# Two quarters of the first Q, K, V projection at new widths, and two attention chunks turned by DMA one phase earlier

## The chip, the cores and the metric

The kernel runs on one core of a Trainium2 chip. A time is device microseconds (us) of one execution of the whole program on that core; a kernel's time is the median of several executions. The engines of the core are named as the profile names them: TensorE is PE, with its weight loads listed apart as PEld; VectorE is DVE; ScalarE is ACT; GpSimd is POOL; SyncE, which here only issues DMAs, is SP. POOL issues DMAs too. Each engine takes its instructions in the order in which they were issued, and waits for the data of the one at its head.

## What is computed

A layer of local, dilated attention (32 heads of 20, eight keys at distances 0, 2, ..., 14) times a gate from a feed-forward network, on a sequence of 2048 rows of 640 in float32:

```python
def reference(A_x, A_wqkv, A_wo, B_x, B_w1, B_w2):
    x = A_x                                   # 1 x 2048 x 640
    xn = _layernorm(x)
    # s: Q, K, V = xn @ wqkv; 32 heads of 20; each row attends to rows
    #    pos - 0, 2, ..., 14; softmax over these eight; result @ wo
    s = _A_ref(xn, A_wqkv, A_wo)
    # _B_ref: silu(xn @ w1) @ w2, with 1536 hidden
    g = _silu(_B_ref(xn, B_w1, B_w2))
    return x + s * g
```

## The kernel before

**Tiling.** The 2048 rows are worked in four groups of 512, g = 0 to 3: two halves of the sequence, and in each the even and the odd rows, since keys lie at even distances. A group is four tiles of 128 tokens (t = 0 to 3). 640 inputs are five K-chunks of 128 (c = 0 to 4). Float32 products are made of three matmuls each: every operand is split into a rounded part (hi) and the rest (lo), and PE computes hi x hi, lo x hi and hi x lo (L971 to L973 in the projection, L1016 and L1018 for products with two column parts of 384 and 256, L1143 to L1145 for `w1`).

**A group's two phases.** In the *Q, K, V phase* (`qkv_phase`) PE makes the projection in four quarters q of eight heads: each is 5 chunks x 4 tiles x 3 = 60 matmuls into four accumulator banks, as wide as the quarter's columns. A quarter's own columns are 160 of Q, 160 of K and 160 of V, 480 together. In the groups g = 1 to 3 the quarters 0, 1 and 2 take 32 columns each of quarter 3's Q besides, so their widths are 512, 512, 512 and 384; in g = 0 all four are 480 wide. Function `parts` says which columns a quarter takes. ACT reads the banks out (`evac_qkv`: keys and values L749, Q L752, the 32 further columns L755), SP shifts keys and values along the rows (`halo`, L767, L777, L779), and DVE makes the scores (L792, L795) and the weighted values (L826, L831, L834) of the attention, which runs on into the next phase. In the *FFN phase* (`ffn_phase`) PE makes `w1` blocks (`up`) and `w2` blocks (`down`) in turn, and somewhere in it the product of the **previous** group's attention with `wo` (`wo_phase`), whose banks DVE reads out by multiplying them into the gate (L1048) before a block of `w2` can use them. The same phase loads the next group's rows of `x` (L615), takes their statistics (L622, L624) and normalizes them (L634).

**Weights.** Seven weight tiles `w` are used in a ring. At first use a weight comes raw from memory by SP (`raw_load`, L546), ACT makes the hi part (L581), POOL or DVE the lo part (L585), and for later groups both halves are stored to memory (L589); from then on POOL loads them in one DMA (L572). The store of quarter 3 of g = 0 is cut: 32-column pieces go to the halves of quarters 0 to 2, since the later groups use them there.

**Turning the attention's output.** `wo_phase` needs the attention's output O with its columns on the partitions. A chunk c of 128 columns is turned by PE, or by DMA in `turn_o`: *send* is a copy on ACT that parts the halves of each word (L676) and two DMA transposes on SP (L680); *join* puts them together on ACT (L689), makes hi on ACT (L693) and lo on DVE (L694). The table `ON_DMA` says for each group which chunks go by DMA, at which quarter of the next Q, K, V phase send and join are issued, and how many us behind by the planner's clock. A send needs two tiles of 128 x 512 to work in: `LENT` lends it the key and value tiles KV[1], KV[2], KV[3] for chunks 1, 2 and 3, between the use of one group and the next (`spare`, `lend`); chunk 0 uses the tiles `turn` and `sf`. Chunks of the next group's x are turned in the same way in the FFN phase (`turn_x`).

**What sets the order.** All operations are handed to a planner (`Weave`) with their reads and writes, a cost from its own table, a priority (mostly the clock of PE when they were handed over) and sometimes an earliest time. It plays them through and fixes one order for each engine; `emit` issues that. So an edit at one place moves instructions at others. The names of the tables that the change touches are `LENT`, `IN_PARTS` and `ON_DMA`; `QAT` is the column at which a ring tile of g = 0's projection begins.

## Time and profile before

| what | us |
| --- | --- |
| median of 3 runs (623.55 to 623.58) | 623.56 |
| the profiled execution | 624.1 |
| its span, first to last instruction | 622.3 |
| PE busy in it | 617.2 |
| DVE busy | 540.7 |
| ACT busy | 272.7 |
| POOL busy | 114.8 |
| granted TensorE clock, mean | 1.000 |

The span is what the trace shows, from the first instruction to the last; the rest of an execution's time lies around it. Busy times of engines overlap, so they do not add up. A timeline row of the profile gives the start in us from the span's begin, the length in us, the engine, the line of the kernel's text, the operation, the tiles that it writes and reads, their shapes and how often it came in a row; in brackets stands how long the engine had been idle before it and for whom it waited. SPq and POOL's DMA rows show the issuing of a transfer, not its landing.

### The profile page before, as it was taken

What the parts mean: (1) busy time and instruction counts of PE and PEld (TensorE: products, weight loads), DVE (VectorE), ACT (ScalarE), POOL (GpSimd) and SP (SyncE); (2) the same over time, 40 slices, a digit from 0 to 9 for tenths busy, and PEclk for the clock granted to TensorE, in tenths of its full rate; (3) what the DMA queues carried; (4) which work ended last, traced back from release to release, by engine and by line L of the source; (5) the groups of instructions that cost most, each with busy time, mean ns of one, the idle gap of its engine ahead of it and who ended that gap; (6) DMA issues with size and microseconds to landing.
All of it is one profiled execution on the core that took longest, in us unless ns stands there. A gap on an engine that the chain in (4) does not pass through costs nothing.

```text
span 622.3 us, 9038 instructions
## 1 busy us (share of the span) xinstructions
PE 617.2 (99%) x3395; PEld 557.9 (90%) x3395; DVE 540.7 (87%) x545; ACT 272.7 (44%) x496; POOL 114.8 (18%) x165
## 2 busy tenths in 40 slices
PE   9999999999999999999999999999999999999997
PEld 7888999998889998999888999989988999999997
DVE  6599899999788998998948499899996999899834
ACT  5445555364545225453545521625654272252220
POOL 5800000011110142111221015121222211111100
PEclk9999999999999999999999999999999999999999
DMA  9999999599999999965999999998499999987552
GB/s 297 305 319 317 323 377 364 220 326 269 278 298 309 331 237 321 272 198 140 203 219 262 344 363 330 295 230 252 137 225 286 240 321 304 295 241 243 189 191 86
DMA packets 105114, 167.39 MB, mean 269 GB/s; under 512 B 36605, under 2 KB 66781, under 8 KB 105069
## 3 DMA queue, kind: packets, MB, share of 16 engines
q1 hardware_dynamic: 78573, 87.08, 52.8%
q0 software_dynamic: 25952, 79.31, 46.6%
q8 instruction: 27, 0.44, 0.3%
q10 hardware_dynamic: 544, 0.41, 0.2%
q14 instruction: 18, 0.15, 0.1%
HBM read 107.91 MB, written 34.16 MB: 228 GB/s over the span
## 4 chain that ended last, share of the span: by engine, by line
PE 98%; DMA 0%; DVE 0%; issue 0%
PE acc L1016 22%; PE acc L1018 15%; PE acc L973 10%; PE acc L971 10%; PE acc L972 10%; PE rot L1144 9%; PE rot L1145 9%; PE rot L1143 9%; PE acc L909 2%; PE rot L644 1%; DMA xin<-in_A_x_dram 0%; PE rot L893 0%; PE rot L1129 0%; DVE st L878 0%; PE rot L852 0%; DVE gate L1097 0%
## 5 line engine op out<-in xcount | busy, mean ns | idle before, releaser
L1016 PE MATMUL acc<-w,sh 128*128 128x384 f32 x384 | 113.4, 334 | 0.0
L971 PE MATMUL acc<-w,th 128*128 128x512 f32 (+2 forms) x300 | 112.9, 376 | 0.0
L973 PE MATMUL acc<-w,th 128*128 128x512 f32 (+2 forms) x300 | 112.8, 376 | 0.0
L972 PE MATMUL acc<-w,tl 128*128 128x512 f32 (+2 forms) x300 | 112.8, 376 | 0.0
L1018 PE MATMUL acc<-w,sh 128*128 128x256 f32 x384 | 107.3, 279 | 0.0
L792 DVE TENSOR_TENSOR pr<-q,kv 128x2560 f32<-128x2560 f32 x32 | 90.3, 2822 | 16.0 <-DMA kv<-kv 15.7
L826 DVE TENSOR_TENSOR pr<-q,kv 128x2560 f32<-128x2560 f32 x32 | 94.5, 2954 | 0.7
L1143 PE MATMUL rot<-th,w 128*128 128x512 f32 x240 | 94.2, 393 | 0.0
L1145 PE MATMUL rot<-th,w 128*128 128x512 f32 x240 | 93.8, 391 | 0.0
L1144 PE MATMUL rot<-tl,w 128*128 128x512 f32 x240 | 93.7, 391 | 0.0
L795 DVE TENSOR_REDUCE l<-pr 128x128 f32<-128x2560 f32 x32 | 90.1, 2815 | 0.3
L1156 ACT ACTIVATE sh<-rot 128x512 fp32r<-128x512 f32 x48 | 28.8, 600 | 139.7 <-PE rot L1145 139.5
L572 POOL DMA_DIRECT2D w<-half_q x52 | 37.4, 719 | 234.4 <-DVE pr L831 97.2
L572 POOL DMA_DIRECT2D w<-half_w x72 | 38.6, 536 | 202.7 <-PE acc L1018 87.9
L831 DVE TENSOR_TENSOR pr<-pr 128x1280 f32<-128x1280 f32 x64 | 74.0, 1156 | 1.3
L1018 PEld LDWEIGHTS acc<-w,sh 128*128 128x128 f32 x384 | 72.2, 188 | 1.1 <-DVE gate L1048 0.3
L1016 PEld LDWEIGHTS acc<-w,sh 128*128 128x128 f32 x384 | 72.1, 188 | 0.9
L972 PEld LDWEIGHTS acc<-w,tl 128*128 128x128 f32 x300 | 56.3, 188 | 8.8
L973 PEld LDWEIGHTS acc<-w,th 128*128 128x128 f32 x300 | 56.3, 188 | 8.7
L971 PEld LDWEIGHTS acc<-w,th 128*128 128x128 f32 x300 | 56.3, 188 | 8.7
L1016 PE MATMUL acc<-w,sl 128*128 128x384 f32 x192 | 57.9, 333 | 0.0
L749 ACT ACTIVATE kv<-acc 128x320 f32<-128x320 f32 x64 | 27.5, 441 | 60.9 <-PE acc L973 59.5
(115 smaller groups left out, 1037.8 us busy)
## 6 DMA issues: line engine op xcount, KB each, us to landing
w<-half_w POOLq DMA_DIRECT2D x72, 640.0 KB, 6.6
w<-half_q POOLq DMA_DIRECT2D x39, 512.0 KB, 5.5
half_w<-w SPq DMA_DIRECT2D x24, 640.0 KB
kv<-kv SPq DMA_DIRECT2D x15, 560.0 KB
w<-half_wo POOLq DMA_DIRECT2D x10, 640.0 KB, 8.0
kv<-kv SPq DMA_DIRECT2D x15, 420.0 KB
gate<-in_B_w_dram SPq DMA_DIRECT2D x16, 320.0 KB
w<-half_q POOLq DMA_DIRECT2D x13, 384.0 KB, 7.6
```

The source lines that it names most:

```text
L572: add("POOL", 1.0, lambda: nc.gpsimd.dma_start(both, src), [("half", u), ("half", u, "more")], [kh, kl], due + 10, nbytes=2 * n * P * 4)
L792: dve(2560, lambda t=t: nc.vector.tensor_tensor(out=PR, in0=win(qq[:, t:t + 2, :], W, 0), in1=win(kv[:, 0, t:t + 2, :], W, CQ), op=OP.mult ...
L795: dve(2560, lambda t=t: nc.vector.tensor_reduce(out=l[:, t:t + 2].rearrange("p t w h -> p (t w h)"), in_=PR.rearrange("p t w (h d) -> p (t ...
L826: dve(2560, lambda t=t, v=v: nc.vector.tensor_tensor(out=PR.rearrange("p t w (h d) -> p t (w h) d", d=DH), in0=e[:, t:t + 2].rearrange("p ...
L971: nc.tensor.matmul(o, hi, wh, start=c == 0, stop=False)
L972: nc.tensor.matmul(o, lo, wh, start=False, stop=False)
L973: nc.tensor.matmul(o, hi, wl, start=False, stop=c == DC - 1)
L1016: nc.tensor.matmul(a[t][0][:, :CA], st, w[:, :CA], start=first, stop=last)
L1018: nc.tensor.matmul(b[t // 2][0][:, h * CB:(h + 1) * CB], st, w[:, CA:], start=first and h == 0, stop=last, skip_group_check=True)
L1143: nc.tensor.matmul(h, wh[:, cs], TH[i][:, c, :], start=c == 0, stop=False)
L1144: nc.tensor.matmul(h, wh[:, cs], TL[i][:, c, :], start=False, stop=False)
L1145: nc.tensor.matmul(h, wl[:, cs], TH[i][:, c, :], start=False, stop=c == DC - 1)
```

## The change

Four things are changed.

1. In the first group the third quarter takes 32 columns of the last quarter's Q, so its widths are 480, 480, 512 and 448. `parts` and `evac_qkv` say so; `SLOT` gives where the 32 columns lie (the first slot of quarter 3's Q tile is now that of quarter 2). Raw loads of these two quarters become two DMAs for each of five chunks (the 32 or 128 Q columns apart); the stores of 32-column pieces fall from nine to six, and the start column `QAT` holds for quarters 0 and 1 alone. ACT has four more readouts of 32 columns.
2. `LENT` becomes a table by group: for the attention that is joined in g = 2 chunk 0 is lent KV[0] in place of `turn` and `sf`.
3. `EARLY_O`: the send of chunks 0 and 1 of g = 1's attention, which was issued at the beginning of g = 2's Q, K, V phase, is issued in g = 1's FFN phase behind its `wo_phase`, no earlier than 48 and 56 us after the planner's clock there; `ON_DMA` now has only their joins, at quarter 0 instead of quarter 1.
4. `IN_PARTS` 3: in the last group the third tile of `x` for the residual is loaded in two DMAs. The argument `NG` in place of `g` in the last group's `turn_o` selects the same tiles as before.

```diff
-LENT = None, 1, 2, 3, None
+LENT = {2: (0, 1, 2, 3, None)}
+EARLY_O = {1: ((0, 48.0), (1, 56.0),)}
-IN_PARTS = 2
+IN_PARTS = 3
+SLOT = 1, 2, 0
@@ parts(i)
-        if i >= first_q:
-            if q < NQ - 1:
-                cols.append(((NQ - 1) * CQ + q * MORE, MORE))
-            else:
-                cols[0] = (q * CQ + q * MORE, CQ - q * MORE)
+        if q == NQ - 1:
+            gone = MORE * (NQ - 1 if i >= first_q else 1)
+            cols[0] = (q * CQ + gone, CQ - gone)
+        elif i >= first_q or q == NQ - 2:
+            cols.append(((NQ - 1) * CQ + SLOT[q] * MORE, MORE))
@@ start(i)
-        return QAT if i < first_q else 0
+        return QAT if i < 2 * DC else 0
@@ raw_load(k)
-            if i >= first_q:
+            if len(cols) > 3 or q == NQ - 1:
@@ turn_o
-        lent = LENT[c] if g < NG - 1 else None
+        lent = LENT[g][c] if g in LENT else None
@@ evac_qkv
-        skip = MORE * q if g and q == NQ - 1 else 0
+        skip = MORE * (q if g else 1) if q == NQ - 1 else 0
-        if g and q < NQ - 1:
+        if q < NQ - 1 and (g or q == NQ - 2):
+            slot = SLOT[q]
             act(MORE, lambda: nc.scalar.activation(
-                Q[NQ - 1][:, t, q * MORE:(q + 1) * MORE], ps[:, 3 * CQ:], AF.Copy), [kp], [("q", NQ - 1, t, q)], 0)
+                Q[NQ - 1][:, t, slot * MORE:(slot + 1) * MORE], ps[:, 3 * CQ:], AF.Copy), [kp], [("q", NQ - 1, t, slot)], 0)
@@ ON_DMA
-              NG - 2: ({0: ((0, 0, 4.0), (1, 0, 4.0)), 1: ((0, 1, 8.0), (1, 1, 8.0), (2, 0, 0.0), (3, 0, 10.0)), 2: ((2, 1, 4.0),), 3: ((3, 1, 0.0),)},
+              NG - 2: ({0: ((0, 1, 2.0), (1, 1, 4.0)), 1: ((2, 0, 0.0), (3, 0, 10.0)), 2: ((2, 1, 4.0),), 3: ((3, 1, 0.0),)},
@@ ffn_phase, behind wo_phase
                     for v in sorted(set(lent)):
                         lend(*v, True)
+                    for c, at in EARLY_O.get(g, ()):
+                        turn_o(g + 1, c, ix, True, False, clock[0] + at)
```

PE's order keeps its rows; only the widths of 120 matmuls differ. A row below is line, operation, tile written and tile read, and the shape. The lines of the changed text are higher by 1 to 5.

SP in the Q, K, V phase of g = 2, from the first shift of quarter 0's keys (kv_93 to kv_96 are the quarters 0 to 3) on. Before:

```order
L767 DMA kv_93<-kv_93 112x2x640
L767 DMA kv_93<-kv_93 15x2x640
L767 DMA kv_93<-kv_93 112x2x480
L680 DMA_TRANSPOSE sf<-turn 128x4x128
L767 DMA kv_93<-kv_93 14x2x480
L777 DMA kv_94<-carry_121 1x2x640
L680 DMA_TRANSPOSE kv_96<-kv_96 128x4x128 x2
```

Of the change:

```order
L770 DMA kv_93<-kv_93 112x2x640
L770 DMA kv_93<-kv_93 15x2x640
L770 DMA kv_93<-kv_93 112x2x480
L770 DMA kv_93<-kv_93 14x2x480
L780 DMA kv_94<-carry_121 1x2x640
L782 DMA kv_94<-carry_121 2x2x480
L682 DMA_TRANSPOSE kv_96<-kv_96 128x4x128 x2
```

The transpose of chunk 0 that stood between the shifts is gone; those of chunk 3 (kv_96) stay.

The same queue at that phase's end, with the loads of `x` for g = 3 (xin) and raw loads of `wo` (xr). Before:

```order
L767 DMA kv_95<-kv_95 112x2x480
L767 DMA kv_95<-kv_95 14x2x480
L777 DMA kv_96<-carry_121 1x2x640
L779 DMA kv_96<-carry_121 2x2x480
L546 DMA xr_107<-in_A_wo_dram 128x640
L615 DMA xin<-in_A_x_dram 128x640
L546 DMA xr_108<-in_A_wo_dram 128x640
L615 DMA xin<-in_A_x_dram 128x640 x3
L589 DMA half_wo_167<-w_77 128x1280
```

Of the change:

```order
L617 DMA xin<-in_A_x_dram 128x640
L780 DMA kv_96<-carry_121 1x2x640
L782 DMA kv_96<-carry_121 2x2x480
L770 DMA kv_95<-kv_95 112x2x640
L770 DMA kv_95<-kv_95 15x2x640
L770 DMA kv_95<-kv_95 112x2x480
L770 DMA kv_95<-kv_95 14x2x480
L617 DMA xin<-in_A_x_dram 128x640 x3
L548 DMA xr_107<-in_A_wo_dram 128x640
L591 DMA half_wo_167<-w_77 128x1280
L548 DMA xr_108<-in_A_wo_dram 128x640
```

One load of `x` moved ahead of quarter 2's shifts (kv_95), the other three ahead of both raw loads.

DVE at the beginning of g = 2's FFN phase, from the normalization to the gate on `wo`. Before:

```order
L634 TENSOR_SCALAR xin<-xin,mv,sd 128x640 x4
L792 TENSOR_TENSOR pr<-q_98,kv_94 128x2560
L795 TENSOR_REDUCE l_104<-pr 128x128
L792 TENSOR_TENSOR pr<-q_98,kv_94 128x2560
L795 TENSOR_REDUCE l_104<-pr 128x128
L1048 TENSOR_TENSOR gate<-acc_113,gate 128x384
```

Of the change:

```order
L636 TENSOR_SCALAR xin<-xin,mv,sd 128x640 x4
L1161 TENSOR_TENSOR sl_87<-sf,sh_84 128x512
L795 TENSOR_TENSOR pr<-q_98,kv_94 128x2560
L587 TENSOR_TENSOR w_81<-xr_108,w_81 128x640
L798 TENSOR_REDUCE l_104<-pr 128x128
L829 TENSOR_TENSOR pr<-q_97,kv_93 128x2560
L834 TENSOR_TENSOR pr<-pr 128x2x640
L834 TENSOR_TENSOR pr<-pr 128x2x320
L837 TENSOR_TENSOR o<-pr 128x2x160
L829 TENSOR_TENSOR pr<-q_97,kv_93 128x2560
L1051 TENSOR_TENSOR gate<-acc_113,gate 128x384
```

One of the two score pairs of quarter 1 moved ahead of the normalization, and two products of quarter 0's values, the first with its sums, ahead of the gate.

SP in the first group, where quarters 2 and 3 are loaded raw. Before:

```order
L546 DMA xr_108<-in_A_wqkv_dram 128x3x160
L767 DMA kv_93<-kv_93 112x2x480
L767 DMA kv_93<-kv_93 14x2x480
L546 DMA gate<-in_A_wqkv_dram 128x3x160 x2
L546 DMA xr_107<-in_A_wqkv_dram 128x3x160
```

Of the change:

```order
L548 DMA xr_108<-in_A_wqkv_dram 128x3x160
L550 DMA xr_108<-in_A_wqkv_dram 128x32
L770 DMA kv_93<-kv_93 112x2x480
L770 DMA kv_93<-kv_93 14x2x480
L548 DMA gate<-in_A_wqkv_dram 128x3x160
L550 DMA gate<-in_A_wqkv_dram 128x32
L548 DMA gate<-in_A_wqkv_dram 128x2x160
L550 DMA gate<-in_A_wqkv_dram 128x128
L548 DMA xr_107<-in_A_wqkv_dram 128x2x160
L550 DMA xr_107<-in_A_wqkv_dram 128x128
```

Each load of the two quarters now has a smaller one behind it.

More of the change, by code (lines that the diff above doesn't have):

```diff
@@ L1213, in ffn_phase @@
                     for c in range(2):
-                        turn_o(g, c, io, True, True)
+                        turn_o(NG, c, io, True, True)
                     free_for(XP, [("xin", t, c) for t in range(T) for c in (0, CA)])
```

## The prediction

> **What bounds the kernel now.** I read the page's busy shares and chain first, then tables by stretch for TensorE (PE), then its waits, then the queues that feed the one stall that they show. Groups are counted g = 0 to 3.
>
> ```profile
> span 622.3 us, 9038 instructions
> PE 617.2 (99%) x3395; PEld 557.9 (90%) x3395; DVE 540.7 (87%) x545; ACT 272.7 (44%) x496; POOL 114.8 (18%) x165
> PE 98%; DMA 0%; DVE 0%; issue 0%
> ```
>
> PE is busy in 617.2 of 622.3 us and is 98% of the chain that ended last. So a gain must come from matmuls that take less time, or from the few gaps between them; work on other engines counts only where PE waits for it. The profiled execution took 624.1 us, 1.8 more than its span, and the median of the runs is 623.56; I work out differences inside the span and put them on the median.
>
> **First term, the widths.** These are four stretches of the table by windows for PE alone (start:end, length, busy and count, granted clock, DMA share, GB/s), each one quarter of a Q, K, V phase with 60 matmuls: 480, 512, 512 and 384 columns.
>
> ```profile
> 47.89:60.85 12.96, 12.96 (x62) 1.00 1.10 316
> 158.29:171.89 13.60, 13.60 (x62) 1.00 1.30 290
> 310.44:324.04 13.60, 13.60 (x61) 1.00 1.43 224
> 337.64:348.07 10.43, 10.43 (x62) 1.00 1.20 296
> ```
>
> Per matmul that is 12.96/60 = 216.0 ns at 480, 226.7 at 512 and 173.8 at 384. From 384 to 512 a column costs 52.9/128 = 0.413 ns; on that line 480 would take 213.5, so the measured 216.0 lies 2.5 ns above it. The change puts 512 and 448 in place of 480 and 480, for 60 matmuls each. The 512 is measured in the other groups. For 448 no row exists. On the line between 384 and 512 it takes 200.2 ns (12.01 us); with the surplus of 480 it takes 202.7 (12.16 us). The pair before is 25.92 us; after, 13.60 + 12.01 = 25.61 or 13.60 + 12.16 = 25.76, a gain of 0.31 or 0.16. If what makes 480 slow belongs to the first group and not to the width, 512 pays it too and the gain is 0. I take 0.23, midway between the first two, since the 512 and 384 of the other groups both lie on one line, and keep 0 to 0.31.
>
> [...]
>
> **Second term, a stall in the third group.** The next table, by windows for all engines, has three blocks of 72 `w2` matmuls, the first from g = 1 and the others from g = 2; then one row of the waits of PE's weight loads, and PE's timeline.
>
> ```profile
> 245.30:255.63 10.33, 10.33 (x73) 10.33 (x72) 10.26 (x9) 8.65 (x10) 3.43 (x4) 1.00 1.09 240
> 375.99:387.04 11.05, 11.01 (x74) 10.75 (x73) 10.98 (x11) 2.19 (x3) 7.35 (x9) 1.00 1.08 353
> 397.25:407.58 10.33, 10.33 (x73) 10.33 (x72) 10.19 (x7) 4.08 (x5) 1.59 (x3) 1.00 1.17 226
> ```
>
> ```profile
> PEld acc L1018 <- DVE gate L1048: 0.3, 1, 0.3
> 377.15 0.33 PE L1016 MATMUL acc<-w,sh 128*128 128x384 f32 x1
> 377.52 0.38 PE L1018 MATMUL acc<-w,sh 128*128 128x256 f32 x1
> ```
>
> Equal work takes 10.33 us twice and 11.05 once, so 0.72 us is lost after 375.99. At 377.15 to 377.52 the pipeline breaks because an accumulator bank is not yet free: VectorE (DVE) must first read the `wo` result out of it (the gate, L1048). The rest of the 0.72 is a slower pitch until the block's end; it began with the break, and I count it to it. Why is the gate late? DVE's timeline (start, length, operation, and in brackets idle time before it):
>
> ```profile
> 328.40 2.83 DVE L792 TENSOR_TENSOR pr<-q,kv 128x2560 f32<-128x2560 f32 x1 [10.07 <-DMA kv<-kv]
> 351.79 0.49 DVE L622 BATCH_NORM_STATS2 st<-xin 128x6 f32<-128x320 f32 x1 [4.83 <-DMA xin<-in_A_x_dram]
> 356.72 0.89 DVE L622 BATCH_NORM_STATS2 st<-xin 128x6 f32<-128x320 f32 x2 [1.58 <-DMA xin<-in_A_x_dram]
> 358.51 0.67 DVE L1158 TENSOR_TENSOR sl<-sf,sh 128x512 fp32r<-128x512 f32 x1
> 359.23 1.51 DVE L585 TENSOR_TENSOR w<-xr,w 128x640 fp32r<-128x640 f32 x2
> 360.86 2.25 DVE L634 TENSOR_SCALAR xin<-xin,mv,sd 128x640 f32<-128x640 f32 x4
> 371.59 2.82 DVE L795 TENSOR_REDUCE l<-pr 128x128 f32<-128x2560 f32 x1
> 374.33 3.14 DVE L1048 TENSOR_TENSOR gate<-acc,gate 128x384 f32<-128x384 f32 x6
> 378.06 2.81 DVE L826 TENSOR_TENSOR pr<-q,kv 128x2560 f32<-128x2560 f32 x1
> 381.40 2.34 DVE L831 TENSOR_TENSOR pr<-pr 128x1280 f32<-128x1280 f32 x2
> 383.77 0.49 DVE L834 TENSOR_TENSOR o<-pr 128x320 f32<-128x320 f32 x1
> ```
>
> DVE stood idle 10.07 us for the shifted keys of quarter 0 and 4.83 and 1.58 us for the next group's rows of `x`; its order then puts two scores (L792, L795) between the normalization (L634) and the gate. Both waits come from the one queue of SyncE (SP):
>
> ```profile
> 311.10 3.44 SPq L767 DMA_DIRECT2D kv<-kv  x3
> 314.58 1.91 SPq L680 DMA_TRANSPOSE sf<-turn  x1
> 316.54 1.53 SPq L767 DMA_DIRECT2D kv<-kv  x1
> 339.94 2.51 SPq L767 DMA_DIRECT2D kv<-kv  x2
> 344.30 0.69 SPq L615 DMA_DIRECT2D xin<-in_A_x_dram  x1
> 347.85 0.33 SPq L546 DMA_DIRECT2D xr<-in_A_wo_dram  x1
> 348.22 2.75 SPq L615 DMA_DIRECT2D xin<-in_A_x_dram  x3
> ```
>
> A transpose of attention chunk 0 stands ahead of the last shift of quarter 0 (316.54), which lands some 10 us after its issue ends. The `x` loads stand behind a raw load of `wo` at 347.85.
>
> The change takes the transposes of chunks 0 and 1 out of this phase, so the four shifts stand together, and its new order has all four `x` loads ahead of that raw load. I follow both chains. *Shifts:* without L680's 1.91 us the fourth ends its issue near 315.9. Its landing has no row; before it took 328.40 - 318.07 = 10.3 us, so it is at latest near 326.2 if that stays, earlier as fewer transposes are in flight. *Loads of x:* the first is now ahead of quarter 2's shifts, the other three right behind them. Those end at 342.45, so the three are issued by 342.45 + 2.75 = 345.2 instead of 350.97. DVE, waiting, began the first tile's statistics 6.8 us behind its issue's end (351.79 - 344.99); with that the last tile's run from 352.0 to 352.9, and with a weight split (0.75) and a few operations under half a us the normalization starts near 354.5 instead of 360.86. *Behind it,* by the new order, come L634 2.25, one L1158 0.67, scores 2.83 and 2.82 with a split 0.75 between, values 2.81, 2.34, 0.49, 2.81: 17.8 us. The gate starts near 372.3. It must start by about 374.33 - 0.72 - 0.23 = 373.4 if PE, itself 0.23 earlier, is not to wait. That holds with 1.1 us to spare, so the term is 0.72, with 0 as its lower bound if that slack is used up.
>
> **The rest at nothing.** Moved, not removed, are two ScalarE (ACT) copies, four transposes, two joins on ACT and two subtractions on DVE; PE's count stays. They now share the DMA engines with the weight loads of g = 1's FFN. The ring of seven weight tiles, loaded as each comes free, hides that; PE's waits name no DMA. If that cover were gone, a load behind one transpose could cost PE up to the 1.91 us of its issue. The third `x` load of the last group in two parts (IN_PARTS) lies long ahead of its use. At the end of the last value product DVE's L1158 goes ahead of both L831:
>
> ```profile
> 590.58 0.60 ACT L855 ACTIVATE th<-rot 128x512 fp32r<-128x512 f32 x1 [2.81 <-PE rot L852]
> 591.21 0.69 DVE L856 TENSOR_TENSOR tl<-rot,th 128x512 fp32r<-128x512 f32 x1 [0.53 <-ACT th L855]
> ```
>
> DVE waits there 0.53 us for ACT, so a delay of up to 0.5 hides; I allow 0 to 0.15.
>
> **Sum.** -0.23 - 0.72 = -0.95, so 623.56 - 0.95 = **622.6 us** (-0.15%). With both terms at their best -1.03; a change of under 0.2% (1.25 us, about what a measurement of this kernel can tell from none) is the likeliest.
>
> **Rivals.** *The stall stays.* If the three `x` loads issue or land over 1.1 us later than I say, part of the 0.72 stays; wholly, only the widths pay: 623.3. For it speaks the thin slack. If the shifts land no earlier than 328.40, the new order is worse than the old: 47 us of DVE work (the new order's operations at their durations before) stand between that score and the gate, it starts at 375.4, and PE loses 1.1 more: 624.4. Against that speaks the transpose gone from the queue.
>
> [...]
>
> *Slower: the first group's loads.* Quarters 2 and 3 of g = 0 come raw from memory, now in two DMAs for each of ten K-chunks. ACT takes what it does in order, and its evacuation of PE's banks stands behind a weight copy:
>
> ```profile
> 33.32 0.61 ACT L581 ACTIVATE w<-gate 128x480 fp32r<-128x480 f32 x1 [1.70 <-DMA gate<-in_A_wqkv_dram]
> 34.15 0.30 ACT L752 ACTIVATE q<-acc 128x160 f32<-128x160 f32 x1
> 27.36 1.45 SPq L546 DMA_DIRECT2D gate<-in_A_wqkv_dram  x2
> 30.92 0.55 SPq L546 DMA_DIRECT2D gate<-in_A_wqkv_dram  x1
> ```
>
> That copy already waits 1.70 us for its load. The first bank is read out at 34.45. Quarter 2 starts at 60.85 - 2 x 12.96 = 34.93 and needs that bank six matmuls later, at 36.23: 1.8 us of slack. SP issues such a load in 0.55 to 0.72 us, and two to four small pieces now stand ahead of the copy's data, so 1.1 to 2.9 us; SP's gaps take some of it, and PE loses 0 to 1.1, of which I take 0. It decides the sign at 1.8 + 0.95 = 2.8 us of delay, and makes the kernel slower by over 0.2% at 4.0: 624.9 us with a landing delayed by 4.1. The splits of later chunks shift with it; PE's waits name none of those on DVE, so I price none.
>
> [...]
>
> *Slower: lent tiles.* Chunks 0 and 1 now sit in the key and value tiles of quarters 0 and 1 until the next phase's start. ACT first writes quarter 0's at 308.60, and two small operations of the softmax, the first at 302.66, are where DVE now has the join's subtractions:
>
> ```profile
> 308.60 0.44 ACT L749 ACTIVATE kv<-acc 128x320 f32<-128x320 f32 x1 [2.98 <-PE acc L973]
> 309.12 0.20 ACT L755 ACTIVATE q<-acc 128x32 f32<-128x32 f32 x1
> ```
>
> ```profile
> 302.66 0.42 DVE L801 TENSOR_TENSOR l<-l,mask 128x256 f32<-128x256 f32 x1
> ```
>
> So some 3.5 us are left (one join stands directly behind it, one a little later). The bank read out by 309.32 is needed six matmuls into quarter 1, at 310.44 + 1.36 = 311.8, which gives 2.5 more. It decides at 3.5 + 2.5 + 0.95 = 7 us of delay, and the time is 625.0 if the joins come 8.4 late.
>
> **Chances.** Forecast 0.54 (own range 622.3 to 623.0); stall stays in part or whole 0.2 (623.0 to 623.6, and to 624.4 with late shifts); widths nothing 0.06; first group's loads 0.1; lent tiles 0.05; a gain above 1.25 us by something that I do not see, such as DVE's earlier work closing other gaps, 0.05. Faster by over 0.2% is that last and the low edge of the forecast: 0.17. Slower by over 0.2%: most of the two slower rivals, 0.13. Within: 0.70. The range that leaves out 2 in 10 is 622.2 to 624.3.
>
> **What would show it.** The two quarters now 512 and 448 wide take 13.60 and 12.0 to 12.2 us. The third group's first `w2` block takes 10.33 us and the wait of L1018's weight load on the gate is gone; the gate starts before 373.4; the score's wait of 10.07 us is shorter; the last three `x` loads are issued by 346. Wrong it is if that block still takes 11 us, if 448 takes as much above the line as to use up 512's share, or if PE shows a gap near 36 us or near 312 us.

## The result, and the profile after

| | runs | median us | lowest to highest us |
|---|---|---|---|
| before | 21 | 623.75 | 623.37 to 628.79 |
| changed | 21 | 633.41 | 625.18 to 639.53 |

The change made the kernel slower. The ratio is 1.0083 with a 95% interval of 1.0064 to 1.0103. That ratio leaves out runs over 1.5% above the fastest of the same kernel, and here such runs belong to the kernel itself; the ratio of the two medians in the table is 1.0155. The changed kernel's 21 runs lie in two bunches: 6 between 625.2 and 626.9 us, 15 between 629.4 and 639.5. The profiled execution, 639.5 us, is the longest of them.

The profile page of the changed kernel: its span, the busy shares and the chain that ended last.

```profile
span 637.7 us, 9053 instructions
PE 624.0 (98%) x3395; PEld 562.3 (88%) x3395; DVE 542.6 (85%) x545; ACT 272.1 (43%) x501; POOL 117.5 (18%) x165
PE 68%; DMA 14%; SPq 5%; issue 5%; DVE 4%; POOL 2%; ACT 2%; DVEq 0%; ACTq 0%; POOLq 0%
```

Before, PE was 98% of the chain. Now DMA transfers and the queue that issues them hold 19% of it. PE's count is the same, but its span grew by 15.4 us (637.7 - 622.3). Next, six blocks of the changed kernel from the table by windows (start:end, length, busy and count for PE, PEld, DVE, ACT, POOL, granted clock, DMA share, GB/s): in the first group the first `w1` block of 45 matmuls and the `w2` block behind it; in g = 2 the first `w2` block (the prediction's second term) and the `w1` block behind it; then a `w1` and a `w2` block of g = 2 some 42 us further on.

```profile
61.35:76.85 15.50, 12.14 (x46) 9.50 (x45) 13.42 (x12) 7.53 (x16) 0.00 (x0) 0.89 1.06 289
76.85:84.05 7.20, 7.20 (x50) 7.20 (x49) 6.26 (x6) 3.31 (x5) 0.00 (x0) 1.00 1.05 397
382.03:392.37 10.34, 10.34 (x74) 10.33 (x72) 8.73 (x9) 4.17 (x5) 2.34 (x4) 1.00 1.07 351
392.37:403.56 11.19, 10.81 (x48) 8.30 (x47) 5.85 (x5) 6.56 (x8) 3.69 (x5) 1.00 1.08 363
434.47:448.79 14.32, 12.14 (x47) 9.52 (x46) 12.65 (x9) 2.96 (x4) 2.37 (x4) 0.88 1.47 142
448.79:463.43 14.64, 12.00 (x74) 11.74 (x72) 6.57 (x10) 10.64 (x15) 1.94 (x3) 0.88 0.85 161
```

The same blocks before, by the same table, took 10.25, 6.94, 11.05, 10.21, 10.24 and 10.34 us. So the first group lost 5.25 + 0.3 us, with 0.5 ahead of it; g = 2 gained 0.71 where the prediction expected it and lost 0.98 + 4.08 + 4.30. The last `wo` product at the end of the kernel adds 0.62, which was not followed further. Together these are 15.3 of the 15.4 us. The waits of PE say what it waited for in the long blocks:

```profile
PE rot L1146 <- ACT sf L1160: 5.9, 3, 3.4
PE acc L1019 <- ACT sh L1159: 2.6, 1, 2.6
```

Both name ACT's silu of the hidden layer (`sh`, `sf`). No wait of PE names a DMA, as before; but ACT's own row is behind one, as the next two parts show.

**First group.** ACT's timeline around the first silu (start, length, operation, idle time ahead of it and what ended that), before and then changed:

```profile
64.65 0.60 ACT L1156 ACTIVATE sh<-rot 128x512 fp32r<-128x512 f32 x1
65.62 0.74 ACT L581 ACTIVATE w<-xr 128x640 fp32r<-128x640 f32 x1
```

```profile
68.53 0.74 ACT L583 ACTIVATE w<-xr 128x640 fp32r<-128x640 f32 x1 [2.60 <-DMA half_q<-w]
70.57 0.60 ACT L1159 ACTIVATE sh<-rot 128x512 fp32r<-128x512 f32 x1
```

The weight copy out of `xr` stood behind the first silu; the planner's new order has it ahead. It waits 2.60 us until a store of an earlier weight (`half_q`) has left the tile that it writes, and the silu starts at 70.57 instead of 64.65.

**Third group.** The queue of SP in g = 2's FFN before, then changed, with POOL's timeline of the changed kernel:

```profile
392.46 0.34 SPq L1061 DMA_DIRECT2D xr<-in_A_x_dram  x1
396.10 2.50 SPq L680 DMA_TRANSPOSE kv<-turn  x2
410.63 5.69 SPq L680 DMA_TRANSPOSE gate<-gate  x4
422.01 2.58 SPq L680 DMA_TRANSPOSE gate<-turn  x2
```

```profile
395.20 2.80 SPq L682 DMA_TRANSPOSE kv<-turn  x2
401.06 0.34 SPq L1064 DMA_DIRECT2D xr<-in_A_x_dram  x1
419.93 9.71 SPq L682 DMA_TRANSPOSE gate<-gate  x3
429.69 7.30 SPq L682 DMA_TRANSPOSE gate<-turn  x2
```

```profile
407.47 0.53 POOL L574 DMA_DIRECT2D w<-half_w  x1 [2.92 <-PE acc L1021]
415.24 4.22 POOL L1065 TENSOR_TENSOR xr<-xr,gate 128x640 f32<-128x640 f32 x1 [7.24 <-DMA xr<-in_A_x_dram]
419.41 2.32 POOL L574 DMA_DIRECT2D w<-half_w  x4
```

Two rows changed place. The row load of `x` for the residual (L1061, now L1064) stands behind two transposes instead of ahead of them, and POOL's addition on it (L1065) has come two weight loads earlier. POOL, which needs the rows, begins 14 us after their issue and has waited 7.24 us, and four weight loads that were due meanwhile leave together at 419.41, just as six transposes begin. The first five then take 17.0 us on the queue, 3.4 each; before, six took 8.3, 1.4 each. What they write is needed by ACT's joins, which stand ahead of the silu:

```profile
440.61 1.36 ACT L691 ACTIVATE xin<-gate 128x1024 uint16<-128x1024 uint16 x1 [12.90 <-DMA gate<-gate]
442.54 0.58 ACT L1159 ACTIVATE sh<-rot 128x512 fp32r<-128x512 f32 x1
452.51 1.34 ACT L691 ACTIVATE xin<-gate 128x1024 uint16<-128x1024 uint16 x1 [8.91 <-DMA gate<-turn]
```

That is one profile, and its chain of causes is a reading. The experiments test it.

### The profile page after: what moved, and what is told of

The parts are those of the page before. It is cut to its first block, busy times and chain, and to the rows that moved or that the text cites. A ratio compares the mean times of both kernels' runs of the same rounds, so it can differ in the third digit from the quotient of the medians.

```text
span 637.7 us, 9053 instructions
## 1 busy us (share of the span) xinstructions
PE 624.0 (98%) x3395; PEld 562.3 (88%) x3395; DVE 542.6 (85%) x545; ACT 272.1 (43%) x501; POOL 117.5 (18%) x165
## 4 chain that ended last, share of the span: by engine, by line
PE 68%; DMA 14%; SPq 5%; issue 5%; DVE 4%; POOL 2%; ACT 2%; DVEq 0%; ACTq 0%; POOLq 0%
PE acc L1019 17%; PE acc L1021 12%; PE acc L976 7%; PE acc L974 7%; PE acc L975 7%; PE rot L1146 6%; PE rot L1148 6%; PE rot L1147 6%; DMA half_wo<-w 3%; DMA gate<-turn 3%; SPq L682 3%; DMA kv<-kv 3%; DMA half_q<-w 2%; DMA xr<-in_A_wqkv_dram 1%; DMA gate<-in_B_w_dram 1%
## 5 line engine op out<-in xcount | busy, mean ns | idle before, releaser
L1019 PE MATMUL acc<-w,sh 128*128 128x384 f32 x384 | 114.7, 337 | 2.6 <-ACT sh L1159 2.6
L974 PE MATMUL acc<-w,th 128*128 128x512 f32 (+3 forms) x300 | 112.9, 376 | 0.0
L976 PE MATMUL acc<-w,th 128*128 128x512 f32 (+3 forms) x300 | 112.9, 376 | 0.0
L975 PE MATMUL acc<-w,tl 128*128 128x512 f32 (+3 forms) x300 | 112.8, 376 | 0.0
L795 DVE TENSOR_TENSOR pr<-q,kv 128x2560 f32<-128x2560 f32 x32 | 90.3, 2821 | 17.0 <-DMA kv<-carry 10.3
L1146 PE MATMUL rot<-th,w 128*128 128x512 f32 x240 | 96.1, 400 | 5.9 <-ACT sf L1160 5.9
L1148 PE MATMUL rot<-th,w 128*128 128x512 f32 x240 | 95.0, 396 | 0.0
L1147 PE MATMUL rot<-tl,w 128*128 128x512 f32 x240 | 95.0, 396 | 0.0
L829 DVE TENSOR_TENSOR pr<-q,kv 128x2560 f32<-128x2560 f32 x32 | 91.9, 2871 | 0.8
L1019 PEld LDWEIGHTS acc<-w,sh 128*128 128x128 f32 x384 | 72.9, 190 | 3.8 <-ACT sh L1159 2.9
L1021 PEld LDWEIGHTS acc<-w,sh 128*128 128x128 f32 x384 | 73.0, 190 | 0.8
L1146 PEld LDWEIGHTS rot<-th,w 128*128 128x128 f32 x240 | 45.7, 191 | 16.4 <-ACT sf L1160 7.1
```

Source lines behind the costliest of these rows:

```text
L795: dve(2560, lambda t=t: nc.vector.tensor_tensor(out=PR, in0=win(qq[:, t:t + 2, :], W, 0), in1=win(kv[:, 0, t:t + 2, :], W, CQ), op=OP.mult ...
L829: dve(2560, lambda t=t, v=v: nc.vector.tensor_tensor(out=PR.rearrange("p t w (h d) -> p t (w h) d", d=DH), in0=e[:, t:t + 2].rearrange("p ...
L974: nc.tensor.matmul(o, hi, wh, start=c == 0, stop=False)
L975: nc.tensor.matmul(o, lo, wh, start=False, stop=False)
L976: nc.tensor.matmul(o, hi, wl, start=False, stop=c == DC - 1)
L1019: nc.tensor.matmul(a[t][0][:, :CA], st, w[:, :CA], start=first, stop=last)
```

## The experiments

In every table, "over 628" counts the runs of the kernel above 628 us. The kernel before ran beside each batch: medians 623.86 to 623.93, over 16 to 29 runs. With its 21 runs of the first table, 5 of its 131 runs lie above 628. The ratio is taken as in the first table.

### The two halves of the change apart

`widths_alone` has only the widths (the diff's part 1). `early_alone` has only the lent tiles and the early transposes (parts 2 and 3; the widths of before). `IN_PARTS` stays at 2 in both (part 4 was not run alone; `after_pool` below holds it).

```diff
@@ widths_alone                    @@ early_alone
+SLOT = 1, 2, 0                    +LENT = {2: (0, 1, 2, 3, None)}
 parts, start, raw_load,           +EARLY_O = {1: ((0, 48.0), (1, 56.0),)}
 evac_qkv as in the change          ON_DMA, turn_o as in the change
```

> The widths of the first group alone; all else as before. Theory 1 (first group: the queue of SP has no slack there, so ten more loads make weight copies on ACT late and the silu behind them holds PE): the quarter pair 512 and 448 takes 25.6 to 25.8 us, and the first w1 block of 45 matmuls, 10.25 us before and 15.5 in the changed kernel's profile, takes 11 to 16 us, not the same in each run; time 624 to 629 us, scattered. Theory 2 (all of the loss comes from the third group's early transposes): 623.3 us, no scatter, first w1 block 10.25.

> Chunks 0 and 1 sent one phase earlier, widths as before (and the third x load in two parts is left as before). Theory 1: no loss in the first group, the third group's w2 block at 10.33 instead of 11.05, and the loss late in the third group's FFN (4.1 us in a w1 block and 4.3 in a w2 block of the changed kernel's profile) either is there too, which makes it a consequence of the early sends: 623 to 631, scattered; or it was only brought on by the first group's delay: 622.8. Theory 2: all of the loss is here, 625 to 639.

| | runs | median us | lowest to highest | over 628 | ratio, interval |
|---|---|---|---|---|---|
| widths_alone | 6 | 627.15 | 625.38 to 629.41 | 3 | 1.0057 (1.0040 to 1.0074) |
| early_alone | 12 | 626.94 | 623.67 to 635.19 | 6 | 1.0023 (0.9999 to 1.0048) |

So there are two losses. The widths cost 3.3 us in the median and 1.5 in the shortest run. The early transposes cost next to nothing in one half of the runs (six at or below 624.6) and 5 to 11 us in the other (six from 629.3 on). That fits the two bunches of the whole change. The profile of `early_alone`, at 632.4 us, shows the stall of the third group alone. POOL waits 4.45 us for the rows and then issues two weight loads together, from 407.70 on; next come SP's queue and the wait of PE.

```profile
408.21 6.51 SPq L681 DMA_TRANSPOSE gate<-gate  x3
414.77 12.69 SPq L681 DMA_TRANSPOSE gate<-turn  x2
```

```profile
PE acc L1017 <- ACT sh L1157: 5.3, 1, 5.3
```

### First group: the loads or the order?

Two causes could stand behind the 3.3 us: the ten further loads on SP's queue, or the place of the weight copy on ACT. `two_loads` keeps the order of before exactly and only splits the raw loads of quarters 2 and 3 into two DMAs. `widths_one_load` has the widths with quarter 3 (480 columns, of which 448 are used) loaded in one DMA.

```diff
@@ two_loads, raw_load
-            nc.sync.dma_start(dst, src)
+            if u[0] == "q" and i < first_q and u[1] >= 2:
+                nc.sync.dma_start(dst[:, 1:], src[:, 1:])
+                nc.sync.dma_start(dst[:, 0], src[:, 0])
@@ widths_one_load, raw_load
+        one = i < first_q and u[0] == "q" and u[1] == NQ - 1
+        if one: n = 3 * CQ
...
-        raws[i] = r, kr
+        raws[i] = (r[:, MORE:] if one else r), kr
```

> The kernel before with the same order on every engine, but each raw load of quarters 2 and 3 of the first group issued as two DMAs (160 columns of Q apart, 640 bytes a row), the same bytes in all. Theory 1 (ten more DMAs on SP's queue): the first w1 block takes 11 to 14 us and the time is 624 to 627. Rival (it is the new order on ACT, or the rows of 128 bytes, that cost): 623.6 and 10.25 us.

> The widths alone, in the same order on every engine as that kernel, but the last quarter's raw weights come in one DMA of 480 columns (32 of them unused) instead of two of 320 and 128: five DMAs fewer. Theory 1: the loss in the first group falls by about half against the widths alone, time 623.3 to 626. Rival (order on ACT): as the widths alone.

`two_loads`: median 626.87 of 8 runs, ratio 1.0042 (1.0026 to 1.0057). `widths_one_load`: 626.55 of 6 runs, 1.0038 (1.0025 to 1.0051). With no other instruction moved, ten more loads cost 3.0 us. `widths_one_load`, with five loads fewer than `widths_alone`, was expected to lose half as much; it lost 2.7, and the 0.6 between the two is within the scatter of six runs each. In the profile of `two_loads`, of a run at 625.55, the first `w1` block takes 11.33 us (10.24 before). PE waits at the first silu here too, 0.8 us, though ACT's order is that of before: a weight copy ahead of it waits for a raw load that comes late on the same queue, and the silu starts at 67.72.

```profile
65.66 0.74 ACT L585 ACTIVATE w<-gate 128x640 fp32r<-128x640 f32 x1 [1.54 <-DMA xr<-in_B_w_dram]
```

Are these loads dear because of their number or because the rows of five of them are short (32 columns are 128 bytes; the other five load 128 columns)? `small_rows` is the kernel before with five further loads of 128 x 32 that nothing uses. `widths_single` has the widths with no load more than before; its quarter 2 loads four pieces of 128 columns that are not the quarter's own, so it computes other Q, K and V.

```diff
@@ small_rows, raw_load
+            if u[0] == "q" and i < first_q and u[1] == 2:
+                nc.sync.dma_start(whole_tile[:, 3 * CQ:3 * CQ + MORE], wqkv[..., 3 * CQ:3 * CQ + MORE])
@@ widths_single, raw_load (over widths_one_load; quarter 2 as 4 x 128 columns)
+            dst = r[:, :4 * P].rearrange("p (s m) -> p s m", s=4)
+            src = wqkv[...].rearrange("p (s m) -> p s m", s=4)[:, :, :P]
```

> The kernel before, same order on every engine, with five unused loads of 128 x 32 behind the third quarter's raw loads of the first group. The two-load kernel had ten more DMAs of 640-byte rows and 626.9 us. If the number of DMAs sets the loss: half of it, 625.2. If rows of 128 bytes cost more than their size: 626.5 or above. If neither: 623.7.

> The widths alone, same order on every engine, with no further load at all: the third quarter's raw weights of the first group come in one DMA of four pieces of 128 columns, the last quarter's in one of 480. The third quarter's columns are not the right ones, so its Q, K and V are left wrong. Theory 1 (the further DMAs on SP's queue are the loss): 623.3 to 623.9 us, first w1 block 10.25 us, scatter as before. Rival (the new order on ACT, weight copies ahead of the readout of banks, does it even without them): 625 to 627, first w1 block above 11. With no stall the pair of quarters also shows what the widths are worth: 25.6 to 25.8 us if my first term holds, 25.9 to 26.1 by the profile of the changed kernel.

`small_rows`: 624.48 of 12 runs, 1.0010 (1.0000 to 1.0020), 0.55 us above before. `widths_single`: 624.78 of 11 runs, one of them at 639.5, 1.0009 (0.9998 to 1.0020). So most of the loss goes when the loads go, and five loads of 128-byte rows cost little by themselves: 0.55 us for five is no more than their number accounts for (ten cost 3.0), so these runs give no sign of a cost of the short rows, and do not tell the two apart. Five loads that nobody waits for cost 0.55 us and ten that the copies need cost 3.0: that fits a queue whose slack is used up first, but a run between the two was not made. A rest of 0.85 us stays in `widths_single` (624.78 - 623.93), above the 623.3 to 623.9 expected. Its profile, of a run at 625.80, shows the new order on ACT at work without the loads: the copy ahead of the first silu still waits 3.31 us for a store, and the first two `w1` blocks take 10.84 and 8.21 us (10.24 and 6.95 before).

The order on ACT was then undone by itself. `widths_act` moved three weight copies behind the readouts and the silu, but left the raw loads where they were, so that some loads replaced a tile before its copy had read it and part of Q, K, V was computed from other chunks; at 634.18 us (6 runs) it says nothing on the question. `widths_act2` moves the loads with the copies, so ACT's order around the first silu is that of before.

```diff
@@ widths_act2, Waves.emit: the planned list, changed before it is issued
+        for tiles, behind, rest in ((on_way[-1:], silu[0, 0], rest_of[0, 0]), (on_way[-3:-1], acts[last], None)):
+            for i in tiles: done.remove(copies[i]); done.remove(rests[i])
...
+            done[k:k] = [copies and rests of tiles]
```

> The widths alone with all their DMAs; only the order on ACT and DVE around the first silu is put back as the kernel before has it (weight tile 78 is copied behind the first silu pair instead of ahead of it, and tiles 76 and 79 behind the readout of the last quarter's banks). Theory 1 (further DMAs make the stores late, and that alone is the loss): 626 to 628 as the widths alone. Theory 1b (the new order puts a copy that waits 3 to 4 us for a store ahead of the silu, and this makes the lateness count): 624 to 625, first w1 block 10.3 to 11.

> The widths alone with all their DMAs; the copies of weight tiles 76, 78 and 79, their subtractions and the loads that need their buffers stand around the first silu as the kernel before has them. The earlier attempt moved the copies without the loads behind them, so that loads overwrote data still to be split; this one keeps that order. Theory 1 (the further DMAs alone are the loss): 626 to 628 as the widths alone. Theory 1b (the copy ahead of the silu, waiting 4 us for a store, makes their lateness count): 624 to 625, first w1 block 10.3 to 11.

`widths_act2`: 626.07 of 6 runs, 625.10 to 627.97, 1.0040 (1.0026 to 1.0053). ACT's timeline:

```profile
64.64 0.60 ACT L1180 ACTIVATE sh<-rot 128x512 fp32r<-128x512 f32 x1 [0.24 <-PE rot L1169]
67.37 0.74 ACT L598 ACTIVATE w<-xr 128x640 fp32r<-128x640 f32 x1 [1.65 <-DMA half_q<-w]
```

The silu is back at 64.64 and the first `w1` block at 10.20 us (11.88 in the profile of `widths_alone`), but the copy still waits for the store, and the second `w1` block takes 7.78 (6.95 before). With the order of before the loads still cost 2.2 us (626.07 - 623.87), not the 0.1 to 1.1 that was expected if the order were the cause. The 1.1 us less than `widths_alone` would be the share of the order, but with six runs each (625.10 to 627.97 against 625.38 to 629.41) it is not clear of the scatter.

### Third group: which row?

Four kernels, all with `early_alone`'s change, moved something near the slow transposes: the joins of ACT to places behind later silus (`early_join`), chunk 2's two transposes behind those of chunks 3 and 4 (`early_sp`), the transposes of chunk 1's second half and chunk 2 behind silu 8 (`early_hold`), and this together with the joins (`early_hold_join`).

```diff
@@ ffn_phase: the planned list, changed before it is issued
+early_join:  joins of chunks 2, 3, 4 go behind silu[NG - 2, 9], [.., 10], [.., 11]
+early_sp:    turned[NG - 2, 2][1:3] go behind turned[NG - 2, 3][1:3] and turned[NG - 2, 4][1:3]
+early_hold:  turned[NG - 2, 1][3:6] + turned[NG - 2, 2][:3] go behind silu[NG - 2, 8]
+early_hold_join: both of early_hold and early_join
```

> The early sends alone, but on ACT (and with them the subtractions on DVE) each of the last three joins of x in the third group stands behind the silu of blocks 9, 10 and 11 instead of ahead of it, as in the kernel before. Theory 3 (the transposes of x land late in some runs, and the joins that wait for them hold up the silu that PE needs): no run above 625, the w2 block of 72 that took 18.15 us takes 10.33. Rival (the transposes are so late that the next Q, K, V phase waits for their data): slow runs of 629 to 635 remain, with the wait in that phase.

> The early sends alone, only SP's order changed: the four transposes of x chunks 3 and 4 in the third group stand together ahead of the two of chunk 2, as in the kernel before, instead of three, two, one. If this split pair is what delays the landing: no run above 625. Theory 3 (the joins' place on ACT): slow runs of 629 to 635 remain, about half of all.

> The early sends alone, but in the third group the join of x chunk 1 and the copy that sends chunk 2 stand on ACT behind the silu of block 8, as in the kernel before, so that four transposes are issued together and two later, instead of six together. Theory 4 (six transposes at once make the landing late): no run above 625, issue of each transpose 1.2 to 1.6 us. If not: slow runs of 628 to 637 remain in half or more.

> As the one before, and the last three joins of x each behind the silu of blocks 9, 10 and 11: around these transposes ACT and SP now have the order of the kernel before. If the loss lies in this stretch of order: no run above 625. If slow runs of 628 to 637 remain, the cause lies ahead of it: what the early sends change before the third group's feed-forward phase.

| | runs | median us | lowest to highest | over 628 | ratio, interval |
|---|---|---|---|---|---|
| early_join | 6 | 633.62 | 625.87 to 637.59 | 5 | 1.0156 (1.0119 to 1.0194) |
| early_sp | 12 | 629.19 | 623.70 to 638.90 | 9 | 1.0043 (1.0021 to 1.0066) |
| early_hold | 12 | 630.73 | 623.52 to 639.98 | 7 | 1.0010 (0.9970 to 1.0050) |
| early_hold_join | 12 | 636.30 | 624.00 to 645.79 | 9 | 1.0046 (0.9997 to 1.0094) |

None of them helped, and each of the readings behind them fell: that the joins stand too early on ACT, that the six transposes go by source as 3, 2, 1 where they went as 4, 2, that too many transposes stand in one stretch. Since the long runs stayed whatever was done with the transposes and their joins, the next two kernels change what stands ahead of them, the two rows above that had changed place: the addition on POOL and the row load on SP. Each was put back alone: in `early_pool` POOL's addition (`late`), in `early_xr` the row load, by moving the two transposes into `kv` behind it.

```diff
@@ early_pool
+        late = x_add[NG - 3, T - 1]
+        done: late goes behind the next two weight loads of POOL
@@ early_xr
+        move = turned[NG - 2, 1][1:3]
+        done: move goes behind x_load[NG - 3, T - 1]
```

> The early sends alone; the one change is on POOL: in the third group the last of the four additions to x (which waits 4.5 us for its rows in the early sends' profile) stands two weight loads later, as in the kernel before, so that these loads are not held up behind it. SP keeps its order. Theory 5 (held-up weight loads are issued in a bunch just as the transposes of x begin, and make these slow): no POOL wait on these rows, transposes issued in 1.2 to 1.6 us each, no run above 625. If not: slow runs of 628 to 640 in half or more.

> The early sends alone; the one change is on SP: the load of those rows stands ahead of the two transposes of x chunk 1, as in the kernel before, instead of behind them. Theory 5: the rows land sooner, POOL's wait shrinks, fewer slow runs. Theory 6 (it is the transposes of chunk 1, started 7 us sooner than in the kernel before, that crowd the queue): transposes start at about 394 us and slow runs vanish too, also where POOL still waits. If slow runs stay at half: neither.

| | runs | median us | lowest to highest | over 628 | ratio, interval |
|---|---|---|---|---|---|
| early_pool | 11 | 624.23 | 623.47 to 625.67 | 0 | 1.0008 (0.9999 to 1.0017) |
| early_xr | 14 | 624.21 | 623.36 to 628.56 | 1 | 1.0006 (0.9997 to 1.0015) |

Either one ends it: 1 run over 628 of 25, against 6 of 12 in `early_alone`, about as often as in the kernel before. (That one, at 628.56, is the profiled run of `early_xr`. Its five transposes take 6.4 us on the queue; what it loses is elsewhere, a wait of PE of 2.4 us at 392.37 for a weight load that POOL issued late.) In `early_xr` the rows are in use 6.6 us after their issue ended; behind the two transposes it was 12.2 us in `early_alone`. In `early_pool` the row load still stands behind the transposes, but POOL's addition is reached after the rows are there, and the weight loads leave one by one (POOL, then SP's queue):

```profile
408.20 0.53 POOL L588 DMA_DIRECT2D w<-half_w  x1 [2.91 <-PE acc L1034]
408.75 1.58 POOL L1079 TENSOR_TENSOR xr<-xr,gate 128x640 f32<-128x640 f32 x1
411.66 0.57 POOL L588 DMA_DIRECT2D w<-half_w  x1 [1.33 <-PE rot L1163]
```

```profile
410.80 4.15 SPq L696 DMA_TRANSPOSE gate<-gate  x3
415.00 2.57 SPq L696 DMA_TRANSPOSE gate<-turn  x2
```

The same five transposes take 6.7 us on the queue, where they took 17.0 in the changed kernel and 19.2 in `early_alone`.

**What separates short runs from long ones.** In six kernels POOL's addition stands in its new place behind the late rows: the changed kernel, `early_alone` and the first four of this part. In all six profiles POOL waits for the rows, two to four weight loads leave together, and the six transposes take 17.0 to 25.0 us on the queue. In the other twelve profiles they take 7.7 to 9.3. Yet one of the six, of `early_hold`, is of a short run, 623.69 us (POOL, then SP's queue):

```profile
407.98 3.86 POOL L1065 TENSOR_TENSOR xr<-xr,gate 128x640 f32<-128x640 f32 x1 [6.70 <-DMA xr<-in_A_x_dram]
411.79 1.63 POOL L575 DMA_DIRECT2D w<-half_w  x3
```

```profile
412.31 12.99 SPq L683 DMA_TRANSPOSE gate<-gate  x4
425.39 3.98 SPq L683 DMA_TRANSPOSE gate<-turn  x2
```

PE waits nowhere behind them. The last transpose ends its issue at 429.4 here, at 431.2 in `early_join`, 433.2 in `early_alone`, 433.8 in `early_sp` and 435.4 in `early_hold_join`, and PE's longest wait behind it is 0, 1.1, 5.3, 6.2 and 7.6 us. So the slow transposes are there in short runs as well, and PE pays for what they are later than it needs them. These are five orders and one run of each; why one execution of a kernel ends the transposes earlier than another was not found.

### The whole change with its causes mended

`after_pool` is the whole change with POOL's addition put back. `after_mended` has, over that, quarter 3 in one load and ACT's order of `widths_act2`.

```diff
@@ after_pool = the change + early_pool's move
@@ after_mended = after_pool + widths_one_load's raw_load + widths_act2's move
```

> The whole change, with the one addition on POOL two weight loads later as in the early sends' kernel. If the change's loss is the sum of the two found: the runs of 630 to 640 go and what is left is the loss of the widths alone, 625.5 to 629. If the third group's loss needs the first group's delay as well or the reverse: some other number, slow runs stay.

> The whole change with all that the runs point to: POOL's addition two loads later, the last quarter's raw weights of the first group in one DMA, and the copies and loads around the first silu in the order of the kernel before. Sum of the parts: five DMAs fewer and the order cost about 1 us each in the widths' kernels, so 624.0 to 625.0; below 623.4 only if the widths or the early sends are worth something that these losses covered.

`after_pool`: 627.31 of 6 runs, 625.73 to 629.07, 1.0052 (1.0034 to 1.0070); `widths_alone` has 627.15. So with that addition put back nothing can be seen any more of what the early transposes cost, and the widths account for the rest. `after_mended`: 625.56 of 12 runs, 624.09 to 628.87, 1.0027 (1.0016 to 1.0039), more than the 624.0 to 625.0 expected. In its profile, that of its longest run, the first two `w1` blocks take 10.20 and 6.94 us, as before; PE waits 2.0 us for the gate in the fourth group, at 529, which was not followed further. So 1.7 us (625.56 - 623.87) of the change's loss stay open. No kernel tried here beats the one before.

## Why the prediction was wrong

It gave 622.6 us, with a range to 624.3; the median is 633.41. By its own steps:

**First term, the widths (-0.23).** The two quarters in question, from PE's table by windows of the changed kernel and of `widths_single`:

```profile
35.31:48.96 13.65, 13.65 (x61) 1.00 0.93 277
48.96:61.35 12.39, 12.39 (x62) 1.00 1.00 293
```

```profile
34.81:48.44 13.63, 13.63 (x62) 1.00 1.09 309
48.44:60.61 12.17, 12.17 (x62) 1.00 0.98 300
```

The 512 came nearly as forecast (13.60). The 448 took 12.39 us in the changed kernel and 12.17 in `widths_single`, where 12.01 to 12.16 was expected. `widths_one_load`, `widths_act2` and `after_mended` agree with `widths_single` (12.16), so without a disturbance the pair is 25.8 against 25.92, a gain of 0.12: the upper value for 448 was right, and the gain is half of what was put in the sum, midway between the forecast's 0.23 and the nothing to which the prediction gave a chance of 0.06.

**Second term, the stall (-0.72).** DVE and SP's queue, changed kernel:

```profile
329.31 2.83 DVE L795 TENSOR_TENSOR pr<-q,kv 128x2560 f32<-128x2560 f32 x1 [5.02 <-DMA kv<-kv]
358.82 2.18 DVE L636 TENSOR_SCALAR xin<-xin,mv,sd 128x640 f32<-128x640 f32 x4
376.36 3.14 DVE L1051 TENSOR_TENSOR gate<-acc,gate 128x384 f32<-128x384 f32 x6
```

```profile
348.25 1.80 SPq L617 DMA_DIRECT2D xin<-in_A_x_dram  x3
```

The mechanism was right in each step. All of this runs 6.04 us late (382.03 - 375.99, the block's starts), which the first group lost. Without that the loads of `x` end their issue at 344.0 (predicted 345.2), the normalization starts at 352.8 (354.5) and the gate at 370.3 (372.3). The score's wait fell from 10.07 to 5.02 us, and the block took 10.34. Its worth was wrong. The term was put on the median, though it was read from one execution that was 0.5 us above it. `small_rows` has before's order in this stretch, and its profile shows no stall either (the block, then the gate):

```profile
375.68:386.01 10.33, 10.33 (x72) 10.21 (x71) 8.70 (x7) 1.19 (x3) 4.97 (x8) 1.00 1.04 372
```

```profile
370.05 3.13 DVE L1051 TENSOR_TENSOR gate<-acc,gate 128x384 f32<-128x384 f32 x6
```

The widths' kernels and `two_loads` have that order too. Of these seven profiles (`widths_act` left out) two have the stall: that of before, with a block of 11.05 us, and that of `widths_act2`, 10.82; in the other five the block takes 10.33 or 10.34. By these, most executions had nothing there to gain.

Nor does the gain last where there is one. `early_pool`, whose gate starts at 370.26 in its profile, is 0.36 us above before (624.23 against 623.87), not 0.72 below. Its block takes 10.34, but the `w1` block behind it 11.05 where it took 10.21 before. The silu there stands behind a copy that waits for POOL, and POOL waits 4.81 us for other rows of `x`:

```profile
388.63 1.06 ACT L692 ACTIVATE gate<-xin 128x1024 uint16<-128x1024 uint16 x1 [7.83 <-POOL xr L1079]
```

The same `w1` block took 11.19 in the changed kernel, but 10.25 in `early_alone`.

**"The rest at nothing."** This is the step that failed most. The ring of weight tiles was named as the cover for the moved transposes, and that "PE's waits name no DMA". Both held in the profile before; neither says how much slack stands behind them. The order shown ahead of the prediction covers SP's queue and DVE in other stretches; the two rows that decided, POOL's addition and the row load some 40 us behind the last row of that group shown, were not read. In half of the runs they cost 5 to 11 us, three to six times the "up to the 1.91 us" that was the price without the cover.

**The rival of the first group's loads (0 to 1.1, taken as 0; chance 0.1).** The queue, the mechanism and the sign were right, the place and the size wrong. It priced the wait at the start of quarter 2, near 36 us, and no profile has one there. The same wait comes one quarter later, at 50.5 us in `widths_alone` (0.4 us) and at 52.3 in `after_pool` (2.1, more than its bound of 1.1): quarter 3 needs a bank of quarter 2, and the last readout of that bank (its 32 further columns) stands on ACT behind a weight copy that waits for its raw load.

```profile
PE acc L989 <- ACT q L773: 2.1, 1, 2.1
```

In the changed kernel most is lost some 30 us behind the place priced, at the silu. "The splits of later chunks shift with it", the prediction says, "so I price none" because PE's waits named none on DVE. The splits on ACT, behind stores and raw loads on that queue, were the ones that mattered.

**The rival of the lent tiles.** Not seen: no wait of PE stands near the beginning of g = 2's Q, K, V phase.

## What to carry to other kernels

A profile shows the waits there are, not the slack behind them: before work is called hidden, follow the queue that it joins to its next in-order consumers and count how late each may come. Where a planner remakes the order, read every row that changes place on every engine, since a load or an addition that no one meant to move can end ahead of something that now holds up the queue. A stall read from a single execution goes into a sum against the median only where a second profile shows it too.

## What the runs showed of the hardware

**Transposes by DMA took longer to issue where weight loads had left in a bunch.** On SP's queue the two into `gate` from `turn` took 2.57 us in `early_pool` and 12.69 in `early_alone`, where POOL had issued two weight loads together half a us ahead of the six transposes; SP's order is the same in both. That the bunch itself does it, and not something else that POOL's wait brings, was not tested apart; in the first of the windows below (`early_alone`) the DMA engines move 64 GB/s at a DMA share of 1.75.

**A wait of 5.3 us cost PE more than its length.** Windows of `early_alone`: one among its transposes, the one in which PE's wait ends (at 446.77), and the next:

```profile
424.00:428.00 4.00, 4.00 (x29) 3.95 (x28) 3.97 (x2) 2.00 (x2) 0.53 (x1) 1.00 1.75 64
...
444.00:448.00 4.00, 1.23 (x4) 1.23 (x5) 0.77 (x2) 3.62 (x5) 0.00 (x0) 0.60 1.22 355
448.00:452.00 4.00, 4.00 (x18) 4.00 (x18) 2.70 (x6) 3.94 (x6) 0.00 (x0) 0.55 0.10 31
```

The granted clock falls to 0.60 and stays at 0.55 in the next 4 us, though PE is busy there: from 447.67 to 449.81 a pair of matmuls of the block comes every 0.53 to 0.54 us, where 72 matmuls in 10.33 us (`before`) make 0.29 a pair. The `w2` block took 18.15 us: 10.33 of work, 5.3 of waiting, and 2.5 more. That the lower clock accounts for all of these 2.5 was not shown.
